# Key weights in four transfers, corrected keys piece by piece, more products on zeros in the last stage, a new order table

## Chip, cores and metric

One core of one Trainium2 chip runs the kernel. The metric is the device time of one execution in microseconds, as the median of several runs.

## What is computed

Two layers, each a linear-attention block A and a sparse gated MLP block B with a residual around each, on x of 2048 rows by 512 columns (bf16). Cut to what matters:

```python
def _A_ref(x, wqkv, wo):                     # H = 32 heads of 16
    q, k, v = split(x @ wqkv)
    phi = lambda t: jnp.where(t > 0, t + 1, jnp.exp(t)) + 1e-6
    pq, pk = phi(q), phi(k)
    kv = jnp.einsum("bhsd,bhse->bhde", pk, v)
    z = jnp.einsum("bhsd->bhd", pk)
    num = jnp.einsum("bhqd,bhde->bhqe", pq, kv)
    den = jnp.einsum("bhqd,bhd->bhq", pq, z)[..., None] + 1e-6
    return (num / den).merge_heads() @ wo

def _B_ref(x, w_r, w_gate, w_up, w_down):
    r = x @ w_r
    idx = jnp.argsort(-r, axis=-1)[:, :2]            # the two rows with the largest logit
    y = (silu(x[idx] @ w_gate) * (x[idx] @ w_up)) @ w_down * sigmoid(r[idx])
    return x with y added to the rows idx

x = A_x
for layer in (1, 2):
    x = x + _A_ref(layernorm(x), A_wqkv, A_wo)
    x = x + _B_ref(layernorm(x), B_w_r, B_w_gate, B_w_up, B_w_down)
```

## The kernel before

The 2048 rows are 16 tiles of 128 rows (`NT`), the 512 columns four pieces of 128 (`NC`). All of x stays on the chip.

**Start.** The host hands in x twice, by rows (`x`) and transposed (`xt`), and the key weights `wk` ([128, 4, 512], 512 KB). `wk` comes in two transfers of 256 KB: pieces 0 and 1 on ScalarE's queue, 2 and 3 on SyncE's. TensorE first runs nine products on a tile of zeros (`spin`, L858) that give nothing but activity. The layer norm's mean is taken out of the key weights, not out of x: `center_keys` multiplies the four pieces of `wk` by a matrix of -1/512 (`nmean`, L872) into one PSUM tile, ScalarE copies it out as `wl` (L875), and four additions give the corrected pieces `wkc` = `wk` + `wl` (L877). Tile 0 doesn't wait for `wkc`: `K_raw(0)` multiplies `xt` by `wk` and adds `xt` by `wl` in the same PSUM tile (L416, L422). From tile 1 on `K_raw` uses `wkc`. Its result is scaled by the row's reciprocal deviation in two passes of ScalarE (`e`, L389, and `rl`, L390), and becomes `pk` by two passes of VectorE or GpSimd. The PSUM tiles of these products ("mm") rotate through three buffers.

**Body.** `G` (L434) sums xn times pk over the 16 tiles in four PSUM tiles, `Q` (L449) makes the queries in 16 groups of four products, `kv` turns the sums into per-head matrices (L488, L500, L530), `den` makes the denominators (L547 to L571), `O` (L587) the block's output, which VectorE adds to x (L592). The two chosen rows of block B of the first layer are worked out beside this (L986 to L1311).

**Last stage.** Once the second layer's x is there, the two rows are searched in parts: the tiles 0 to 11 first (`topk`, L986 to L995), then 12 to 15 (L1438, L1450), then all (L1452). `WL` (L1457) holds weights that pick the two rows; products with it (L1468, L1476) gather them into `xg2`, from which VectorE makes `xoT` and `xs` (L1484). Then come the rows of the output (L1524), gate and up (L1493) and down (L1533), and `yo` (L1546), stored over the two rows by the last two transfers (L1550), which wait for the four stores of the whole output (L1353). Each store takes four tiles of `xo` (written as `pk` in the rows), which are scaled copies of x made by `last_out` on ScalarE (L321), VectorE or GpSimd (L323). In three pauses TensorE multiplies zeros (`hot`, L1406): four, two and three products of 128 by 512.

**Order.** `Plan` records every operation with its engine. The string `ORDER` then lists them two characters each, and the operations are issued in that order, so it fixes the order within every engine and every queue. `PICK` names, for each operation that several engines can do, the one that does it. A GpSimd operation marked `port` waits for the VectorE operation marked `port` that stands last before it in the table; the code adds that wait itself.

## Time and profile before

| | |
|---|---|
| median of 3 runs | 154.9 us (154.62 to 155.18) |
| time of the profiled execution | 154.57 us |
| its span, first to last instruction | 152.9 us |
| TensorE busy | 145.0 us, 95% of the span |
| VectorE busy | 125.7 us, 82% |
| ScalarE busy | 110.3 us, 72% |
| GpSimd busy | 44.8 us, 29% |
| mean granted clock of TensorE | 0.978 |

The profile is of one execution. Busy time of TensorE counts products that overlap, so a full share doesn't mean that none of it could be shorter. The end of a stretch is set by the wait that ends last in it, and the chain of waits follows these back from the last instruction.

### The profile page before, as it was taken

How to read it: one execution, taken by the hardware profiler on the slowest of the kernel's cores; microseconds unless marked ns; L12 is line 12 of the kernel's file. 1: busy time of each engine (PE TensorE's matmuls, PEld its weight loads, DVE VectorE, ACT ScalarE, POOL GpSimd, SP SyncE). 2: the span in 40 equal slices, each digit the busy share in tenths (PEclk: the TensorE clock that was granted, in tenths of full speed). 3: DMA queues.
4: the chain of work that ended last, by engine and by line, in shares of the span. 5: the costliest groups of instructions: out<-in, count | busy, mean ns of one | idle time of the engine just before them, and what ended most of it. 6: DMA issues, size and time to landing. Idle time of an engine off the chain costs nothing.

```text
span 152.9 us, 3774 instructions
## 1 busy us (share of the span) xinstructions
PE 145.0 (95%) x1296; PEld 73.6 (48%) x1313; DVE 125.7 (82%) x455; ACT 110.3 (72%) x268; POOL 44.8 (29%) x102
## 2 busy tenths in 40 slices
PE   7999999999999999999999999999999999997790
PEld 2344444454445444444444455665546554554490
DVE  0499999849798999999999588676499999989930
ACT  3279999697277786798987565133877998989930
POOL 7623514341104442504500031210341144562100
PEclk9999999999999999999999999999999999999965
DMA  4999999959991000379553510000000000040380
GB/s 117 361 265 382 313 299 258 79 108 333 206 321 60 0 4 0 69 130 422 135 109 71 103 34 0 6 0 4 0 0 4 0 4 0 0 137 9 137 274 5
DMA packets 23155, 18.20 MB, mean 119 GB/s; under 512 B 18016, under 2 KB 20576, under 8 KB 22752
## 3 DMA queue, kind: packets, MB, share of 16 engines
q1 hardware_dynamic: 22840, 17.57, 42.6%
q10 hardware_dynamic: 296, 0.39, 0.8%
q8 instruction: 10, 0.16, 0.4%
q14 instruction: 9, 0.07, 0.2%
HBM read 11.67 MB, written 2.10 MB: 90 GB/s over the span
## 4 chain that ended last, share of the span: by engine, by line
PE 74%; DVE 16%; ACT 4%; issue 3%; DVEq 0%; ACTq 0%
PE g L434 17%; PE mm L449 16%; PE g L587 9%; PE mm L402 9%; DVE x L592 7%; PE mm L416 6%; PE tp L858 3%; DVE pq L571 2%; ACT e L389 2%; PE tp L1069 1%; PE g L1493 1%; ACT rl L390 1%; PE g L488 1%; PE g L872 1%; DVE x L1295 1%
## 5 line engine op out<-in xcount | busy, mean ns | idle before, releaser
L371 ACT ACTIVATE e<-mm 128x512 bf16<-128x512 f32 x48 | 28.2, 600 | 12.7 <-PE mm L402 7.1
L434 PE MATMUL g<-pk,xn 128*128 128x512 bf16 x125 | 31.2, 379 | 0.2
L449 PE MATMUL mm<-xnT,wq 128*128 128x512 bf16 x119 | 30.9, 379 | 0.4
L587 PE MATMUL g<-KW,pq 128*128 128x512 bf16 (+2 forms) x129 | 30.1, 372 | 0.2
L607 ACT ACTIVATE sq<-x 128x512 bf16<-128x512 bf16 (+2 forms) x31 | 18.8, 609 | 1.8 <-DVE x L592 1.6
L434 PEld LDWEIGHTS <-xn 128*128 128x128 bf16 x128 | 12.3, 98 | 13.7
L587 PEld LDWEIGHTS <-pq 128*128 128x128 bf16 x132 | 12.3, 98 | 13.3
L449 PEld LDWEIGHTS <-wq 128*128 128x128 bf16 x128 | 11.6, 97 | 13.3 <-issue 0.6
L379 POOL TENSOR_TENSOR pq<-rl,em 128x512 bf16<-128x512 bf16 x7 | 8.1, 1153 | 28.0 <-DVE em L375 23.4
L375 DVE TENSOR_SCALAR em<-e 128x512 bf16<-128x512 bf16 x48 | 13.1, 288 | 3.9 <-ACT e L371 3.6
L402 PE MATMUL mm<-wk,xnT 128*128 128x512 bf16 x63 | 16.0, 379 | 0.1
L416 PE MATMUL mm<-wkc,xt 128*128 128x512 bf16 x59 | 14.3, 379 | 0.1
L334 DVE BATCH_NORM_STATS2 st<-x 128x6 f32<-128x512 bf16 x16 | 10.5, 680 | 4.4 <-DMA x<-in_A_x_dram 4.4
L390 ACT ACTIVATE rl<-mm,rho 128x512 bf16<-128x512 f32 x16 | 11.0, 704 | 1.1 <-issue 1.1
L389 ACT ACTIVATE e<-mm,rho 128x512 bf16<-128x512 f32 x16 | 10.8, 699 | 1.1 <-PE mm L422 1.0
L592 DVE SCALAR_TENSOR_TENSOR x<-x,opr,g 128x512 bf16<-128x512 bf16 (+2 forms) x17 | 11.3, 711 | 0.0
L382 DVE SCALAR_TENSOR_TENSOR pk<-mm,em 128x512 bf16<-128x512 f32 x16 | 11.0, 688 | 0.2
L382 DVE SCALAR_TENSOR_TENSOR pq<-mm,em 128x512 bf16<-128x512 f32 x16 | 10.7, 686 | 0.2
L592 DVE SCALAR_TENSOR_TENSOR x<-x,g 128x512 bf16<-128x512 bf16 x16 | 10.5, 681 | 0.0
L416 PEld LDWEIGHTS <-xt 128*128 128x128 bf16 x64 | 6.3, 98 | 7.9 <-issue 0.7
L374 ACT ACTIVATE rl<-mm 128x512 bf16<-128x512 f32 x16 | 9.1, 596 | 1.3 <-PE mm L449 1.1
L323 POOL TENSOR_SCALAR xn<-x,s,nb 128x512 bf16<-128x512 bf16 x8 | 6.5, 821 | 10.6 <-DVE nb L357 9.9
(294 smaller groups left out, 242.2 us busy)
## 6 DMA issues: line engine op xcount, KB each, us to landing
wgu<-in_B_wgu_dram SPq DMA_DIRECT2D x2, 1408.0 KB, 6.5
out_dram<-pk SPq DMA_DIRECT2D x4, 512.0 KB, 3.0
wd<-in_B_wd_dram SPq DMA_DIRECT2D x1, 1408.0 KB, 6.7
xt<-in_A_xt_dram SPq DMA_DIRECT2D x2, 512.0 KB, 8.1
x<-in_A_x_dram SPq DMA_DIRECT2D x2, 512.0 KB, 9.9
xt<-in_A_xt_dram SPq DMA_DIRECT2D x3, 256.0 KB, 3.7
x<-in_A_x_dram SPq DMA_DIRECT2D x3, 256.0 KB, 4.6
wq<-in_A_wq_dram SPq DMA_DIRECT2D x1, 512.0 KB
```

Of the source, the lines that this page charges most:

```text
L371: act(0.5, lambda: A.activation(out=e()[:], in_=p()[:], func=ACT.Exp), r=[p], w=[e], **k)
L375: dve(0.2, lambda: V.tensor_scalar(out=em()[:], in0=e()[:], scalar1=1.0, scalar2=TINY, op0=ALU.min, op1=ALU.add), r=[e], w=[em], port=True ...
L382: dve(0.6, lambda: V.scalar_tensor_tensor(out=out_ap, in0=p()[:], scalar=0.0, in1=em()[:], op0=ALU.max, op1=ALU.add), r=[p, em], w=[key], **k)
L389: act(0.57, lambda: A.activation(out=e()[:], in_=p()[:], func=ACT.Exp, scale=s_), r=[p, ("rho0", t)], w=[e])
L390: act(0.57, lambda: A.activation(out=rl()[:], in_=p()[:], func=ACT.Relu, scale=s_), r=[p, ("rho0", t)], w=[rl])
L402: T_.matmul(p()[:], lhsT=xnT[:, c, t * P : (t + 1) * P], rhs=wk[:, c, :], start=(c == 0), stop=(c == NC - 1))
L416: T_.matmul(p()[:], lhsT=xt[:, t, c, :], rhs=w_[:, c, :], start=(c == 0), stop=(c == NC - 1 and not raw))
L434: T_.matmul(Gs[c]()[:], lhsT=xn[:, t, gcol(c) : gcol(c) + P], rhs=pk[:, t, :], start=first, stop=last)
L449: T_.matmul(p()[:], lhsT=wq[:, i, c, :], rhs=xnT[:, i, j * D : (j + 1) * D], start=(i == 0), stop=(i == NC - 1))
L587: T_.matmul(p()[:, 0:n], lhsT=pqt(c, t * P, P), rhs=KWs[layer][:, c, a : a + n], start=(c == 0), stop=(c == NC - 1),)
L592: dve(0.07 + 0.6 * n / D, lambda a=a, n=n, p=p, h=h: V.scalar_tensor_tensor(out=x[:, t, a : a + n], in0=x[:, t, a : a + n], scalar=1.0 if ...
L607: A.activation(out=sq()[:, 0:n], in_=xh, func=ACT.Square, scale=float(D) ** -0.5, accum_out=acc)
```

## The change

- `wk` comes in four transfers of 128 KB, one for each piece, alternating between ScalarE's queue (0 and 2) and SyncE's (1 and 3). Each of the four products with `nmean` then needs one piece.
- The seven products on zeros at the start were nine.
- `K_raw(1)` is issued as four products of their own (L424 in the new file), each behind its piece of `wkc`.
- In the last stage the third pause has five products on zeros in place of three, and three more (`hot4`) stand between the gathering products and the output's rows, which name `hot4` as something to come after.
- `ORDER` and `PICK` are new throughout. Across the whole kernel VectorE has three fewer copies out of PSUM (L315, 7 to 4), two fewer of `last_out` (5 to 3), one fewer of each of the norm and the `wkc` additions, two more additions of pq (9 to 11) and one more square with its sum. ScalarE has three more of the copies, GpSimd two more of `last_out` and one `wkc` addition.

The diff, without most of the tables:

```diff
 ORDER = (
-    "0P8b000Q01030R020e05060708090A0X0B0k3x040Y450S0W0V0Z0f0T0a0g0U0b0r0l463y0y0m0c0h0i0n0w0C170s0o0t0z0D0E0H0F1D0G0x"
...
+    "00010R420S4403020406050708090A0B0C0D0E0T0F0G0J8f0Z0U0m0a0n0b0o0c4A0W4B0V0X0g0p0h0Y0t0j0d0u0q0v0i0w1C0x13110y0r12"
...
-    dma(wk[:, 0:2, :], A_wk[:, 0:2, :], [("wk", 0)], 256, eng="ACT")
+    for c in range(NC):
+        dma(wk[:, c : c + 1, :], A_wk[:, c : c + 1, :], [("wk", c)], 128, eng=("ACT", "SP")[c % 2], prio=-70.0 + c)
     x_load(0, 1, eng="ACT")
     xt_load(0, 1, 0.0, prio=-60.0)
-    dma(wk[:, 2:4, :], A_wk[:, 2:4, :], [("wk", 2)], 256, prio=-59.0)
...
+        def f1(c):
+            T_.matmul(p()[:], lhsT=xt[:, t, c, :], rhs=wkc[:, c, :], start=(c == 0), stop=(c == NC - 1))
+        if t == RAW:
+            for c in range(NC):
+                pe(MM, lambda c=c: f1(c), r=[("xt", t), ("wkc", c)], w=[p])
+        else:
+            pe(4 * MM, f, r=[("xt", t)] + r, w=[p])
...
-            pe(2 * MM, lambda k=k: f(k), r=[("wk", k)], w=[p])
+            pe(2 * MM, lambda k=k: f(k), r=[("wk", k), ("wk", k + 1)], w=[p])
...
-    spin(9)
+    spin(7)
...
-    hot(3, ["gE"], "hot3")
+    hot(5, ["gE"], "hot3")
...
-    pe(1.05, f, r=["WL", "onesb", "hot3"] + [("x", t) for t in (*range(LO, NT), "E")], w=[xg2]).st = 0.02
+    pe(1.05, f, r=["WL", "onesb", "hot3"] + [("x", t) for t in (*range(LO, NT), "E")], w=[xg2, "gW"]).st = 0.02
+    hot(3, ["gW"], "hot4", 2)
...
-    pe(0.15, f, r=["xoT", "masks0"], w=[yp])
+    pe(0.15, f, r=["xoT", "masks0", "hot4"], w=[yp])
```

VectorE at the start, before: statistics of the first two tiles (`st`), the four additions for `wkc`, and what follows.

```order
L334 BN_STATS st<-x 128x6 x2
L336 BN_AGGR mv<-st 128x2
L877 TENSOR_TENSOR wkc<-wk,wl 128x512 x4
L357 SCALAR_TENSOR_TENSOR nb<-mv,rho 128x1
L336 BN_AGGR mv<-st 128x2
L831 CAST blockmask<-mm 128x128
```

And now:

```order
L334 BN_STATS st<-x 128x6 x2
L336 BN_AGGR mv<-st 128x2 x2
L837 CAST blockmask<-mm 128x128
L883 TENSOR_TENSOR wkc<-wk,wl 128x512 x3
L357 SCALAR_TENSOR_TENSOR nb<-mv,rho 128x1 x2
```

The second tile's statistics and a mask are now ahead of the additions, of which three are left; the fourth (piece 1) is GpSimd's.

VectorE in the last stage, before: from the weights `WL` to the reciprocal of the gate's sigmoid. L323 are tiles of `xo`, L1484 `xoT` and `xs`, L1002 and L1006 the rows' indices.

```order
L1457 SCALAR_TENSOR_TENSOR WL<-keys,s_193,sc 128x45 x2
L323 TENSOR_SCALAR pk<-x,opr,nb 128x512 x4
L1484 TENSOR_REDUCE xoT<-tp 128x4x2
L1484 TENSOR_REDUCE xs<-tp 128x8
L323 TENSOR_SCALAR pk<-x,opr,nb 128x512
L1002 TENSOR_SCALAR s_194<-s_193 128x2
L1006 SCALAR_TENSOR_TENSOR s_195<-s_194 128x1
L1509 TENSOR_SCALAR s_198<-s_197 128x2
```

And now:

```order
L1463 SCALAR_TENSOR_TENSOR WL<-keys,s_193,sc 128x45 x2
L323 TENSOR_SCALAR pk<-x,opr,nb 128x512
L1008 TENSOR_SCALAR s_194<-s_193 128x2
L1012 SCALAR_TENSOR_TENSOR s_195<-s_194 128x1
L323 TENSOR_SCALAR pk<-x,opr,nb 128x512
L1491 TENSOR_REDUCE xoT<-tp 128x4x2
L1491 TENSOR_REDUCE xs<-tp 128x8
L323 TENSOR_SCALAR pk<-x,opr,nb 128x512
L1516 TENSOR_SCALAR s_198<-s_197 128x2
```

Between `WL` and `xoT` stand two tiles of `xo` and the two index operations, where four tiles of `xo` stood. The two tiles ahead are tiles 12 and 8; the one behind `xs` is tile 9, of the store that is issued last (tiles 8 to 11; before, tiles 12 to 15 were last).

GpSimd at its end, before: halves of the scales (L1343, L1344) and the key of the early candidates (L1431, L1432).

```order
L1343 CAST sc<-rho 128x3
L1344 TENSOR_TENSOR sc<-rho,sc 128x3
L1431 TENSOR_TENSOR s_185<-cand,eyg 128x2
L1432 TENSOR_TENSOR keys<-s_185 128x1
L1620 UNCONDITIONAL_BRANCH
```

And now:

```order
L1349 CAST sc<-rho 128x3
L1350 TENSOR_TENSOR sc<-rho,sc 128x3
L1437 TENSOR_TENSOR s_185<-cand,eyg 128x2
L1438 TENSOR_TENSOR keys<-s_185 128x1
L323 TENSOR_SCALAR pk<-x,opr,nb 128x512
L1627 UNCONDITIONAL_BRANCH
```

A tile of `xo` (tile 11, of the last store) now stands at GpSimd's end. In the table the VectorE operation marked `port` that stands last before it is tile 8 of `xo`.

## Rows read from the trace of the kernel before

**Rows 1.** Windows; columns: stretch, us, busy (instructions) by engine, clock, DMA.
```profile
14.60:116.40 101.80, 101.02 (x808) 50.65 (x820) 86.98 (x304) 74.67 (x177) 26.91 (x45) 1.00 0.48 118
116.40:138.20 21.80, 21.64 (x253) 11.58 (x245) 21.16 (x65) 19.45 (x55) 9.43 (x19) 1.00 0.07 25
138.20:143.90 5.70, 4.17 (x48) 1.75 (x44) 5.53 (x42) 5.40 (x18) 1.40 (x7) 1.00 0.12 39
143.90:149.40 5.50, 4.71 (x161) 4.27 (x161) 2.80 (x14) 2.69 (x5) 0.00 (x0) 0.71 0.74 253
```

**Rows 2.** Chain of waits, in order of time; columns: start us, us, what.
```profile
1.06 4.02 PE tp L858 x9
...
143.89 1.29 DVE pk L323 x4
```

**Rows 3.** Timeline, 0 to 14 us: start, us, engine, line, operation.
```profile
4.97 1.64 PE L872 MATMUL g<-wk,nmean 128*128 128x512 bf16 x4
...
6.44 1.03 PE L416 MATMUL mm<-wk,xt 128*128 128x512 bf16 x4
6.64 0.60 ACT L875 ACTIVATE wl<-g 128x512 bf16<-128x512 f32 x1 [3.61 <-PE g L872]
...
7.27 1.43 DVE L877 TENSOR_TENSOR wkc<-wk,wl 128x512 bf16<-128x512 bf16 x4 [0.33 <-ACT wl L875]
...
8.44 2.85 PE L416 MATMUL mm<-wkc,xt 128*128 128x512 bf16 x12
```

**Rows 4.** DMA issues: tiles, queue, count, KB each, median us to landing.
```profile
out_dram<-pk SPq DMA_DIRECT2D x4, 512.0 KB, 3.0
...
wk<-in_A_wk_dram SPq DMA_DIRECT2D x1, 256.0 KB, 3.9
wk<-in_A_wk_dram ACTq DMA_DIRECT2D x1, 256.0 KB, 4.1
```

**Rows 5.** Timeline, 112 to 134 us.
```profile
115.56 0.69 DVE L375 TENSOR_SCALAR em<-e 128x512 bf16<-128x512 bf16 x3
...
116.19 0.41 PE L547 MATMUL tp<-pq,Z 128*32 128x128 bf16 x16
...
118.89 0.68 DVE L315 CAST KW<-g 128x512 bf16<-128x512 f32 x1
...
133.27 0.77 POOL L323 TENSOR_SCALAR pk<-x,opr,nb 128x512 bf16<-128x512 bf16 x1
```

**Rows 6.** Timeline, 134 to 153 us.
```profile
140.19 0.40 PE L990 MATMUL tp<-identf,s 128*128 128x128 f32 x2 [0.89 <-DVE s L986]
...
142.64 0.82 PE L1406 MATMUL g<-warm 128*128 128x512 bf16 x3
...
143.80 1.38 DVE L323 TENSOR_SCALAR pk<-x,opr,nb 128x512 bf16<-128x512 bf16 x4
...
144.50 0.24 PE L1476 MATMUL tp<-WL,xt 128*128 128x6 bf16 x4
...
145.35 0.24 PE L1524 MATMUL g<-ident,xoT 128*32 128x128 bf16 x4 [0.62 <-DVE xoT L1484]
...
147.91 1.37 PE L1533 MATMUL g<-wd,h 128*32 128x128 bf16 x44
...
149.33 0.29 DVE L1546 CAST yo<-g 128x128 bf16<-128x128 f32 x1 [1.14 <-PE g L1533]
```

**Rows 7.** Windows of half a microsecond, columns as in Rows 1.
```profile
146.00:146.50 0.50, 0.50 (x26) 0.50 (x23) 0.04 (x1) 0.41 (x2) 0.00 (x0) 0.69 1.03 338
146.50:147.00 0.50, 0.50 (x25) 0.50 (x23) 0.13 (x1) 0.15 (x1) 0.00 (x0) 0.50 1.01 336
```

**Rows 8.** Timeline of SyncE's queue, 145.6 to 150 us.
```profile
145.77 0.37 SPq L1353 DMA_DIRECT2D out_dram<-pk  x1
149.87 0.71 SPq L1550 DMA_DIRECT2D out_dram<-yo  x1
```

**Rows 9.** SyncE's waits: who, for whom, us, times, longest.
```profile
SPq L1550 <- DMA out_dram<-pk: 2.0, 1, 2.0
```

51 lines of the change are left out of this document (25 added, 26 removed).

## The prediction

> **What bounds the kernel now.** I read the windows first, then the chain of waits, then the timelines at both ends, where the chain leaves TensorE. From 14.6 to 116.4 us TensorE is busy for 101.02 of 101.80 us, so at most 0.8 us can be won there without removing products, and the change removes none there. From 116.4 to 138.2 us VectorE is nearly as full (21.16 of 21.80 us) beside a full TensorE, and from 138.2 to 143.9 us VectorE leads (5.53 of 5.70 us). In the last stretch the granted clock is 0.71 on average [rows 1]. The chain begins with the nine products on zeros, 4.02 us from 1.06 us, and near the end it passes through four VectorE tiles of `xo` (L323), 1.29 us [rows 2]. So the parts to price are the start up to the corrected keys, the balance between TensorE and VectorE around 116 us, and the last 6 us.
>
> **The start.** The nine products take 4.02 us, 0.45 us each, and the first product of the means starts at 4.97 us; its four take 1.64 us, and from 6.44 us four products take 1.03 us and twelve 2.85 us, 0.24 us each [rows 2, 3]. By this pace TensorE is at the lower of its two levels (1.2 GHz) until about 6.2 us and at the upper (2.4 GHz) after, though it has worked since 1.06 us. Seven products on zeros end at 1.06 + 7 x 0.45 = 4.2 us. The means can't start before their key pieces land: the two 256 KB transfers land 3.9 and 4.1 us after issue, a 512 KB store in a quiet time takes 3.0 us [rows 4]. So the first two pieces may come as late as before (4.97 us) or a good microsecond sooner. I take a start at 4.3 us, nearer to the early end because only half of the bytes stand before them. That is 0.67 us of TensorE time at half pace, worth 0.33 us of later time if the pace changes where it did; bounds 0 and 0.8.
>
> The Trainium skill (DMA: Bandwidth & Descriptors, Anatomy of one DMA) fits a transfer on the GpSimd path by 2.0 us plus bytes over 436 GB/s: most of it doesn't shrink with the size. By that the first pieces land 0.3 us sooner, and the term is 0.15 us. The 3.9 and 4.1 us here are far above the 2.6 us that the fit gives for 256 KB; no row shows 128 KB of weights.
>
> What follows the means is `wl` (0.60 us on ScalarE, from 6.64 us), then four additions on VectorE from 7.27 us, 1.43 us or 0.36 us each [rows 3]. `wl` comes earlier, but VectorE now does the second tile's aggregation and the mask ahead of the additions, so they begin near 7.2 us all the same. Three take 1.07 us; the fourth, on GpSimd, costs 0.77 us (a one-input pass of that size, [rows 5]) to about twice that, and begins some 0.6 us ahead of VectorE's. The piecewise product of tile 1 hides the rest: before, it began at 8.44 us with the additions ending at 8.70 us, now its first piece is there by 7.6 us and its last by 8.4. If GpSimd's piece holds the others up, the term of 0.33 us is lost. I take -0.35 us for the start in all, the bounds being -0.8 and +0.1. SyncE's queue gets one more issue, but the loads behind it wait for the same bytes as before, and what is moved behind transposes (rows 12 to 15 of x) isn't used for another ten microseconds.
>
> The Trainium skill (SBUF — State Buffer, SBUF: two separate sides) says that GpSimd and a VectorE pass with two SBUF inputs share one port pair, which the first to start holds until it ends. By that GpSimd's addition makes VectorE's three wait, and the start wins nothing. No row here shows the two in such a pass together.
>
> **The body.** Products and their count are the same. Across the kernel VectorE gives away three PSUM copies (0.68 us each, [rows 5]) and gets some back; where TensorE leads, this is worth nothing. In the second layer eight products of `Q`, two groups, are moved behind the last `G`. The sums of `G` are ready 8 x 0.24 = 1.9 us sooner, and so is all of `kv` behind them, less what else is moved ahead of it. Against that stand VectorE's passes for these two groups, which now fall into its full stretch: twice an em of 0.69/3 = 0.23 us [rows 5] and an addition of about 0.4 us, 1.3 us. I take 0 for the body: -0.8 if all of TensorE's idle time there goes, +1.3 if VectorE's passes come on top.
>
> **The last stage.** The two added products of the third pause take 0.43 us at 0.215 us each. The pause is 0.44 us: its three products end at 142.64 + 0.82 = 143.46 us, and the next start behind `WL` at 143.9 us [rows 2, 6]. They are just hidden; if `WL` comes sooner, they cost up to 0.4 us. The three of `hot4` take 0.65 us from about 144.6 us, when the last gathering product has started (144.50 us and three more), so until 145.25 us. The output's rows started at 145.35 us, 0.62 us idle, waiting for `xoT` [rows 6]. `xoT` itself stood behind four tiles of `xo`, 1.38 us; now two tiles (0.69 us) and two index passes (about 0.2 us each), so it is ready 0.3 us sooner. Of this `hot4` leaves 0.1 us.
>
> Behind that the clock matters. It was granted at 0.69 from 146.0 to 146.5 us and at 0.50 after [rows 7], behind pauses of 0.44 and 0.62 us and products of few columns. Earlier in the stage pauses of up to 0.89 us [rows 6], with products on zeros between them, left it at 1.00 [rows 1]. Five more of these in the two pauses should hold it. The 44 products of the down projection took 1.37 us at 0.50; 16 of the same form took 0.41 us at the upper level [rows 5, 6], which makes 44 x 0.41/16 = 1.13 us, and twice the clock can at most halve the 1.37. So the clock is worth 0.24 to 0.69 us there; I take 0.45. The gate and up products have two columns each, for which I take nothing. `yo`, ready at 149.33 + 0.29 = 149.62 us [rows 6], would be ready 0.55 us sooner, at 149.07.
>
> The last transfers wait for the stores as well. The last store was issued at 145.77 us and the last transfer at 149.87 us [rows 8], after 2.0 us in which SyncE waited for stores [rows 9]; so `yo` and the last store came almost together, and `yo` alone gains nothing. The last store now needs tile 9 (VectorE, behind `xs`, about 145.5 us) and tile 11 on GpSimd, 0.77 us [rows 5] behind VectorE's tile 8 (143.9 + 0.35 + 0.4 + 0.35 = 145.0 us), so 145.8 us: issued as before. But the store ahead of it (tiles 12 to 15) is issued sooner, so it may land after 3.0 us [rows 4], at 148.8 us, and not at 149.7. The gain of the stage lies between 0 and 0.65 us; I take 0.35.
>
> **Sum.** -0.35, 0 and -0.35 make -0.7 us. The profiled execution took 154.57 us, 152.9 of it its span; it becomes 153.9. It lies 0.33 us under the median of the runs, 154.9 us, so the median becomes 154.2 us.
>
> **Rivals.**
> - The gains are hidden at both ends: GpSimd's addition delays tile 1, and tile 9 of `xo` waits for GpSimd's tile 11 (to 145.8 + 0.35 us), so the last store lands no sooner than before. For it: `yo` and the store stand together in [rows 8, 9]. Against it: the store's landing depends on the store ahead, which is now earlier. Time: 154.9 less 0.1, 154.8 us. This is what the port rule named above would make of it.
> - Slower, by VectorE after 116 us: the two moved groups of `Q` put 1.3 us of its passes behind `kv`, where it has 0.64 us idle in 21.8 [rows 1]. It decides once `kv` comes less than 1.3 us sooner, for instance since its four PSUM copies now wait in ScalarE's queue. With the full price, the start's 0.35 us kept and nothing from the last store: 154.9 + 1.3 - 0.35 = 155.85, some 155.8 us. Against it: the copies that VectorE no longer does.
> - Faster: the new order also takes out the 0.8 us in which TensorE idles from 14.6 to 116.4 us, or most of it, and VectorE follows with its lighter load: 154.2 less 0.8, 153.4 us. Against it: those 0.8 us are spread over 100 us.
> - The clock falls all the same. Then `yo` is 0.1 us sooner in place of 0.55; the time is 154.45 us, within the forecast's own range.
>
> **Chances.** The forecast, with the case of the clock, 0.43 (its own range 153.6 to 154.8 us); hidden gains 0.18; slower 0.22; faster 0.17. A difference under 0.3%, 0.46 us, can't be told from no change. Faster than 154.44 us: 0.30 of the forecast's 0.43, 0.03 of the hidden, all 0.17, so 0.50. Slower than 155.36 us: 0.19 of the slower case and 0.01 of the rest, 0.20. The same: 0.30. For 8 times in 10 the range runs from 153.0 us (the fast case with the start's better bound in part) to 155.6 us.
>
> **What would show it.** The start is right if the first product of the means begins at 4.2 to 4.4 us and `G`'s first at least 0.3 us sooner than its place before; wrong if TensorE pauses after the seventh product on zeros for more than 0.3 us, or if VectorE's additions wait for GpSimd's. The body is right if VectorE's first addition into x of the second layer stands no later than before against the end of `kv`. The last stage is right if the granted clock is still 1.00 during the down projection, `hot4` ends by the time `xoT` is ready, and the last transfer waits for a store. A median above 155.4 us would make the forecast wrong as such, and so would one under 153.6 us, which would mean that the order and not the named edits moved the time.

## The result and the profile after

The changed kernel is slower: 155.92 us in the median of 16 runs (155.3 to 156.93) against 155.04 us of the kernel before in as many runs beside it (153.85 to 155.61). The ratio is 1.0062, with a 95% interval from 1.0037 to 1.0086. The forecast of 154.2 us and its range (to 155.6 us) are both missed. The profiled execution took 155.49 us and its span 153.7 us, against 154.57 and 152.9 us.

The windows of the changed kernel, columns as in [rows 1]:

```profile
14.60:116.40 101.80, 100.72 (x822) 50.78 (x836) 85.98 (x305) 75.90 (x180) 22.30 (x41) 1.00 0.51 116
116.40:138.20 21.80, 21.64 (x225) 11.31 (x227) 21.42 (x70) 20.12 (x57) 10.86 (x20) 1.00 0.07 25
143.90:149.40 5.50, 4.47 (x164) 3.66 (x160) 2.66 (x12) 2.58 (x5) 0.77 (x1) 0.93 0.57 193
146.00:146.50 0.50, 0.50 (x26) 0.50 (x23) 0.15 (x1) 0.31 (x2) 0.00 (x0) 1.00 1.02 338
146.50:147.00 0.50, 0.50 (x26) 0.50 (x23) 0.21 (x2) 0.19 (x1) 0.00 (x0) 1.00 0.79 246
```

The two long stretches look as they did. In the last 5.5 us the granted clock has risen from 0.71 to 0.93, and where it stood at 0.69 and 0.50 [rows 7] it is 1.00.

The start, on the timeline (start us, us, engine, line, operation):

```profile
1.06 3.17 PE L864 MATMUL tp<-warm 128*128 128x512 bf16 x7 [1.06 <-DVE warm L218]
4.02 1.65 PE L878 MATMUL g<-wk,nmean 128*128 128x512 bf16 x4
5.71 0.60 ACT L881 ACTIVATE wl<-g 128x512 bf16<-128x512 f32 x1 [2.20 <-PE g L878]
5.77 1.04 PE L416 MATMUL mm<-wk,xt 128*128 128x512 bf16 x4
6.39 1.15 POOL L883 TENSOR_TENSOR wkc<-wk,wl 128x512 bf16<-128x512 bf16 x1 [1.14 <-ACT wl L881]
7.57 1.09 DVE L883 TENSOR_TENSOR wkc<-wk,wl 128x512 bf16<-128x512 bf16 x3
8.04 1.05 PE L424 MATMUL mm<-wkc,xt 128*128 128x512 bf16 x4 [0.37 <-DVE wkc L883]
8.92 2.75 PE L416 MATMUL mm<-wkc,xt 128*128 128x512 bf16 x12
```

The means start at 4.02 us (before 4.97) and `wl` at 5.71 (6.64), both some 0.9 us sooner [rows 3]. But VectorE's additions begin 0.3 us later and TensorE waits 0.37 us for them. Tile 1's products (L424) start at 8.04 us; before, they were the first four of the twelve that start at 8.44. So 0.40 us of the 0.9 are left there.

The last stage, on the timeline:

```profile
142.44 1.25 PE L1412 MATMUL g<-warm 128*128 128x512 bf16 x5
143.16 0.51 DVE L1463 SCALAR_TENSOR_TENSOR WL<-keys,s,sc 128x45 bf16<-128x45 f32 x2
144.38 0.81 PE L1412 MATMUL g<-warm 128*128 128x512 bf16 x3
144.70 0.77 POOL L323 TENSOR_SCALAR pk<-x,opr,nb 128x512 bf16<-128x512 bf16 x1 [1.58 <-DVE pk L323]
144.76 0.85 DVE L323 TENSOR_SCALAR pk<-x,opr,nb 128x512 bf16<-128x512 bf16 x1
145.29 1.95 PE L1500 MATMUL g<-xs,wgu 128*128 128x2 bf16 x72
147.57 0.80 PE L1540 MATMUL g<-wd,h 128*32 128x128 bf16 x44
148.42 0.29 DVE L1553 CAST yo<-g 128x128 bf16<-128x128 f32 x1 [0.58 <-PE g L1540]
```

SyncE's queue at the end, its longest wait there, and the times from issue to landing of the four stores:

```profile
145.77 0.37 SPq L1359 DMA_DIRECT2D out_dram<-pk  x1
150.71 0.71 SPq L1557 DMA_DIRECT2D out_dram<-yo  x1
```
```profile
SPq L1557 <- DMA out_dram<-pk: 3.2, 1, 3.2
```
```profile
DMA to landing us min/median/max: 2.9/3.0/4.8
```

The down projection takes 0.80 us in place of 1.37 [rows 6], and `yo` is there at 148.71 us, 0.91 us sooner. Yet the final transfer is issued at 150.71 us, 0.84 us later than before [rows 8]. The last store is issued at 145.77 us in both kernels; its landing took 3.9 us before and takes 4.8 us now, and SyncE's wait for it has grown from 2.0 us [rows 9] to 3.2.

Three marks divide the time: the end of the first layer's last `G` product, about 42 us ("`G` ends" below); the first `WL` pass; the issue of the final transfer. A mark is fair only if both kernels have done the same work up to it. The end of the last key product, about 32 us, is not: the twenty small products with `wr` (L837 and L842 before, L843 and L848 now), 0.5 us, stood behind it and now stand ahead of it. Up to the last `G` product both orders issue the same products, as a count of every TensorE record of e3 and e5 (below) shows. Before, then after:

```profile
33.85 0.54 PE L837 MATMUL mm<-wr,wot 128*128 128x1 bf16 x16
38.66 3.62 PE L434 MATMUL g<-pk,xn 128*128 128x512 bf16 x16
```
```profile
30.94 0.54 PE L843 MATMUL mm<-wr,wot 128*128 128x1 bf16 x16
40.08 1.89 PE L440 MATMUL g<-pk,xn 128*128 128x512 bf16 x8
```

| | `G` ends | to `WL` | `WL` to final issue |
|---|---|---|---|
| before | 42.28 | 101.10 | 6.49 |
| after | 41.97 | 101.19 | 7.55 |
| difference | -0.31 | +0.09 | +1.06 |

So the final transfer's 0.84 us are the last stage alone: in these two executions the start gains 0.31 us and the body loses 0.09.

### The profile page after: what moved, and what is told of

It is laid out like the page before. It is cut to its first block, busy times and chain, and to the rows that moved or that the text cites. A ratio compares the mean times of both kernels' runs of the same rounds, so it can differ in the third digit from the quotient of the medians.

```text
span 153.7 us, 3756 instructions
## 1 busy us (share of the span) xinstructions
PE 144.6 (94%) x1298; PEld 73.1 (48%) x1316; DVE 124.0 (81%) x454; ACT 112.5 (73%) x270; POOL 44.0 (29%) x101
## 4 chain that ended last, share of the span: by engine, by line
PE 76%; DVE 13%; DMA 3%; issue 2%; ACT 2%; ACTq 1%; DVEq 0%
PE g L440 18%; PE mm L455 17%; PE g L593 9%; PE mm L402 9%; PE mm L416 8%; DVE x L598 6%; DMA x<-in_A_x_dram 3%; ACT sq L613 2%; PE tp L1075 1%; DVE pq L577 1%; PE g L494 1%; PE tp L553 1%; PE g L1500 1%; PE g L1412 1%; DVE x L1301 1%
## 5 line engine op out<-in xcount | busy, mean ns | idle before, releaser
L593 PE MATMUL g<-KW,pq 128*128 128x512 bf16 (+2 forms) x129 | 29.6, 372 | 0.3 <-issue 0.2
L375 DVE TENSOR_SCALAR em<-e 128x512 bf16<-128x512 bf16 x48 | 13.6, 294 | 7.7 <-ACT e L371 6.6
L613 ACT ACTIVATE sq<-x 128x512 bf16<-128x512 bf16 (+2 forms) x30 | 18.3, 610 | 1.3 <-DVE x L598 1.1
L416 PE MATMUL mm<-wkc,xt 128*128 128x512 bf16 x56 | 13.5, 379 | 0.0
L598 DVE SCALAR_TENSOR_TENSOR x<-x,g 128x512 bf16<-128x512 bf16 x16 | 10.8, 682 | 0.9 <-PE g L593 0.8
L598 DVE SCALAR_TENSOR_TENSOR x<-x,opr,g 128x512 bf16<-128x512 bf16 (+2 forms) x17 | 11.2, 712 | 0.1
L323 POOL TENSOR_SCALAR xn<-x,s,nb 128x512 bf16<-128x512 bf16 x7 | 5.3, 768 | 19.9 <-DVE em L375 7.6
L577 DVE TENSOR_TENSOR pq<-pq,rd 128x1024 bf16<-128x1024 bf16 x14 | 9.4, 685 | 0.1
L402 PEld LDWEIGHTS <-xnT 128*128 128x128 bf16 x64 | 6.0, 98 | 7.1 <-issue 0.6
```

Source lines behind the costliest of these rows:

```text
L375: dve(0.2, lambda: V.tensor_scalar(out=em()[:], in0=e()[:], scalar1=1.0, scalar2=TINY, op0=ALU.min, op1=ALU.add), r=[e], w=[em], port=True ...
L402: T_.matmul(p()[:], lhsT=xnT[:, c, t * P : (t + 1) * P], rhs=wk[:, c, :], start=(c == 0), stop=(c == NC - 1))
L416: T_.matmul(p()[:], lhsT=xt[:, t, c, :], rhs=w_[:, c, :], start=(c == 0), stop=(c == NC - 1 and not raw))
L577: pl.any({"DVE": (0.6, True), "POOL": (2.25, True)}, lambda e, q=q: EL[e].tensor_tensor(out=q, in0=q, in1=rd()[:].to_broadcast([P, 2, D]), ...
L593: T_.matmul(p()[:, 0:n], lhsT=pqt(c, t * P, P), rhs=KWs[layer][:, c, a : a + n], start=(c == 0), stop=(c == NC - 1),)
L598: dve(0.07 + 0.6 * n / D, lambda a=a, n=n, p=p, h=h: V.scalar_tensor_tensor(out=x[:, t, a : a + n], in0=x[:, t, a : a + n], scalar=1.0 if ...
```

## What held the store

In the stores' tail the trace has a packet of another queue. DMA by queue (packets, MB, share of 16 engines), of the changed kernel from 148.5 to 149 us, then from 149.5 to 150 us:

```profile
GB/s 0 0 1311 0 0 0 0 0 0 0 0 0 0 0 0 0 0 0 0 0 0 0 0 0 0 0 0 0 0 0 0 0 0 0 0 0 0 0 0 0
q8 instruction: 1, 0.02, 11.9%
```
```profile
q1 hardware_dynamic: 4, 0.00, 6.1%
```

The kernel before, from 149 to 149.5 us:

```profile
GB/s 0 0 82 0 0 82 0 0 0 82 0 0 0 1311 0 0 0 0 0 0 0 0 0 0 0 0 0 0 0 0 0 0 0 0 0 0 0 0 0 0
q8 instruction: 1, 0.02, 11.8%
```

Each figure of GB/s is for a fortieth of the window. The large packet, 16 KB of code, holds one DMA engine for 11.9% of 16 x 0.5 us, 0.95 us. Before, it starts at 149.16 us, right behind the last 1 KB packets of the store (82 GB/s). Now it starts at 148.53 us, nothing runs beside it, and the store's last six 1 KB packets follow from 149.46 to 150.0 us, each as the one before it ends. That they wait on the same engine is read from these times; the trace doesn't name a packet's engine.

I had three theories. **A:** TensorE's next piece of code is called when TensorE leaves its last product; a faster last stage calls it sooner. **A2:** the piece is called at a fixed place in TensorE's program, well ahead of its use, and cuts in when TensorE passes that place early against the last store. **B**, the rival to both: the earlier third store or GpSimd's tile 11 slows the last one.

**Products behind the last product** (e1 after, e2 before; A: TensorE stays busy, the piece comes late, the store lands after 3.9 us).

```diff
+    hot(5, [], "hot5")
```

(`hot5` stands last in the table.)

> The changed kernel with five products on zeros (128x512) behind TensorE's last useful product; nothing waits for them. Theory A: TensorE fetches a piece of code when it leaves its last product; in the changed kernel that piece (16 KB on one DMA engine, 0.95 us) starts at 148.55 us, ahead of the last packets of the last store, which then lands at 150.6 instead of about 149.3, and the two final transfers wait for it. Five products take about 1.05 us at full clock, so the fetch starts at about 149.5, behind the store's tail: the final transfers are issued at about 149.3 to 149.4, the profiled span ends 1.2 to 1.4 us earlier than the changed kernel's, and the time is 154.4 to 154.8 against 155.0 of the kernel before. Rival B: the store lands late for a reason of its own (memory, receipt), or what ends last is something else: the time stays at 155.7 to 156.0, the final issue 2 us behind yo. Rival C: the added work at TensorE's end costs by itself: over 156.

> The kernel before with the same five products on zeros behind its last useful product. Theory A: there the code piece starts at 149.16 us, just behind the last packet of the last store (landed 149.67, yo ready 149.62), so there is hardly anything to win: 0 to -0.3 us (the gain only in executions in which the piece comes a little sooner), 154.7 to 155.1. Rival C (work at TensorE's end helps or costs by itself, through the clock or the end of the program): the same shift as in the changed kernel with these products, over 0.7 us either way.

e1 took 156.18 us (ratio to before 1.0085, 1.0053 to 1.0117), its final transfer 7.44 us behind `WL`, the piece again at 148.66 us. e2 took 154.92 us (0.9994, 0.9962 to 1.0025), 6.48 us. (Each ratio is to the kernel before as it ran beside that experiment.) Nothing moved: A is wrong. e1 also shows that the clock is not sure to hold: with the changed kernel's products ahead of it, its down projection was granted 0.50 of the clock and took 1.37 us.

```profile
148.14 1.37 PE L1540 MATMUL g<-wd,h 128*32 128x128 bf16 x44
```

**The named products alone, in the kernel before** (e3, and e4 with `hot5` as well).

```diff
-    hot(3, ["gE"], "hot3")
+    hot(5, ["gE"], "hot3")
...
+    hot(3, [], "hot4")
```

> The kernel before with only the products on zeros of the change: five instead of three in the third pause, three in the new fourth pause; the weights, the start and the order of the rest are as before. Theory A: yo comes 0.5 to 0.8 us sooner since the clock holds, but the code piece of TensorE also comes that much sooner (148.4 to 148.7) and meets the tail of the last store, which is issued at 145.77 as before: it lands at 150.4 to 150.9, so the time gets worse by 0.7 to 1.2 us, to 155.7 to 156.2. Rival B (the late landing belongs to the new order of the stores and of the output tiles): the store lands at 149.7 as before, which was level with yo, and the time is 154.8 to 155.1. What I predicted of these products (-0.35): 154.7.

> The kernel before with the change's products on zeros and, behind TensorE's last useful product, five more. Theory A: the code piece starts at about 149.6, behind the store's tail; the store then lands at 149.3 to 149.7 and ends the wait: 154.7 to 155.1, level with the kernel before or up to 0.3 us below it, and 0.7 to 1.2 us below the same kernel without the five products. Rival B: no difference from that kernel.

e3's `yo` and its final transfer:

```profile
148.63 0.29 DVE L1546 CAST yo<-g 128x128 bf16<-128x128 f32 x1 [0.57 <-PE g L1533]
149.84 0.71 SPq L1550 DMA_DIRECT2D out_dram<-yo  x1
```

`yo` is 0.70 us sooner than before and the transfer leaves as before: 154.71 us, ratio 0.9989 (0.9956 to 1.0021); e4 154.65 us, 1.0002 (0.9964 to 1.0039). The products hold the clock here (1.00 in the down projection, which takes 0.80 us) and it is worth nothing, for the store ends last. By themselves they don't make the store late: so far B stood better than A, which had forecast 155.7 to 156.2 us for e3.

**A2 from both sides.** Between the starts of two successive pieces lie 199 to 399 records of TensorE before and 131 to 408 after, 268 on average in both; one spacing in each is exactly 256 (records 1222 to 1478 before, 686 to 942 after). The Trainium skill (Runtime: NRT & Kernel Launch, Instruction fetch mechanics) says that an engine's code is refilled in blocks of 256 instructions by a DMA queue of its sequencer's own, and that crossing a block's boundary is "mostly hidden". The averages are near the first, and e6 below disagrees with the second as far as a store is concerned: it waits for the piece. If the place is fixed, two things follow that look wrong otherwise: more work on the chain to `yo` should make the changed kernel faster (e5), and splitting products on zeros at the start, 141 us ahead, should make the kernel before slow (e6). The edits of e5, in the changed kernel, and of e6, in the kernel before (36 products of 128 columns for 9 of 512):

```diff
-    hot(3, ["gW"], "hot4", 2)
+    hot(5, ["gW"], "hot4", 2)
```
```diff
-            for _ in range(n):
-                T_.matmul(
-                    p()[:].rearrange("p (a d) -> p a d", a=NC), lhsT=warm[:, 0, :], rhs=warm[:].to_broadcast([P, NC, P]),
...
+            for a in range(4 * n):
+                a = a % 4 * P
+                T_.matmul(p()[:, a : a + P], lhsT=warm[:, 0, :], rhs=warm[:, 0, :], start=True, stop=True)
```

> The changed kernel with five instead of three products on zeros in the fourth pause, 0.45 us more on TensorE's chain. The five products at the program's end did not move the code piece (it started at 159.65 against 159.78 on the trace's own clock), so it isn't called at TensorE's end but from a place inside the last stretch, and it cuts into the last store in the changed kernel (landing 4.8 us) and in that variant (4.7), where the 72 gate products start 0.48 and 0.43 us ahead of the store's issue; where they start 0.12 to 0.2 us ahead (the kernel before and its three variants) the piece comes behind the store's last packet and the landing is 3.9. Theory A2: it is this lead of TensorE over the last store that decides. Two more products take the lead away (0.45 us), the piece falls behind the store, which lands about 3.5 us after its issue, at 149.3; yo is ready at 149.15: 154.5 to 154.9, that is 1.0 to 1.4 below the changed kernel, by adding work to its longest chain. Rival B2: the new order of the stores makes the landing 4.8: 155.8 to 156.1, yo hidden behind it. Rival C: TensorE's chain ends last: 156.3.

> The kernel before with each of its nine products on zeros at the start (128x512) as four of 128x128: the same columns, 54 more TensorE instructions ahead of everything else. Theory A2: pieces of TensorE's code are 256 instructions, so the last piece is called 54 instructions sooner within the gate products, which run at about 27 ns for two instructions, 0.7 us sooner; it then cuts into the last store as in the changed kernel, whose order of stores this kernel does not have: landing 4.6 to 4.9 us instead of 3.9, time 155.7 to 156.1 against 155.0. Rival B2 (order of stores): landing 3.9, 154.9 to 155.2. If the split products take longer at the start, that shows in the first 6 us and is to be taken off.

e5: `yo` is a full microsecond later than in the changed kernel (0.44 us by the two products, 0.57 by a down projection that took 1.37 us at a granted clock of 0.50) and the final transfer 0.93 us sooner.

```profile
149.46 0.29 DVE L1553 CAST yo<-g 128x128 bf16<-128x128 f32 x1 [1.14 <-PE g L1540]
149.78 0.70 SPq L1557 DMA_DIRECT2D out_dram<-yo  x1
```

Its DMA from 148.5 to 149 us shows the piece behind the store's packets again, as before:

```profile
GB/s 0 0 0 0 82 0 0 0 0 0 82 0 0 0 82 0 0 0 82 0 0 82 0 0 0 1311 0 0 0 0 0 0 0 0 0 0 0 0 0 0
q8 instruction: 1, 0.02, 11.8%
```

e5 took 154.82 us, ratio to before 1.0033 (1.0003 to 1.0064), 6.62 us behind `WL`. e6 took 155.8 us, 1.0078 (1.0044 to 1.0111), 7.52 us behind `WL`. Its zeros at the start take the 4.02 us of before, its piece falls into the midst of the last store, from 147 to 147.5 us, and that store lands after 4.9 us (the final transfer leaves at 150.84 us):

```profile
1.06 4.02 PE L859 MATMUL tp<-warm 128*128 128x128 bf16 x36 [1.06 <-DVE warm L218]
```
```profile
q8 instruction: 1, 0.02, 13.9%
```
```profile
DMA to landing us min/median/max: 2.9/3.1/4.9
```

e6 has neither the changed stores nor GpSimd's tile 11 nor a held clock, and it has the whole loss. That is A2, and against B. Since splitting TensorE's products moved the piece, the queue is TensorE's.

Nine kernels have whole stores and no split zeros, and they fall into line by the lead of the gate products' start over the last store's issue: a lead of 0.48 and 0.49 us (after, e1) goes with landings of 4.80 and 4.69 us, 0.24 us (before, e2, e3, e4) with 3.89, and 0.05 us (e5 and, below, e10 and e12) with 3.55 and 3.56. What the traces don't show is the call itself. The piece starts 4.21, 4.98 and 5.37 us behind `WL` in e7 (below), e1 and after, whose TensorE programs are the same up to there, and within 0.02 us of the end of the store's last packet in before, e2, e3, e4, e5, e8, e10 and e12. So its start depends on the stores, and that the place of the call is fixed in the program is argued, not shown.

**Away from the piece.** e18 splits all zeros of the changed kernel, which puts more instructions into the program and other ones where its pieces begin; e7 and e8 send the last two stores as four of 256 KB (e7 in the changed kernel, with tiles 12 and 15 of `xo` exchanged between ScalarE and VectorE; e8 in e3's kernel); e9 adds the split to e7, e14 to e8. The products of `spin` have 92 columns there (45 of 102 in e14), those of `hot` four times 128.

```diff
-    spin(7)
+    spin(39)
```
```diff
-            store(t - 3, t + 1)
+            store(t - 3, t + 1 if t < 11 else t - 1)
...
-    store(LO, NT)
+    store(LO + 2, NT)
...
+    store(10, 12, "o2")
+    store(12, 14, "o2")
```

> The changed kernel with its last two stores (tiles 12 to 15, 8 to 11) as four of two tiles each, issued as their tiles are ready (12 and 13, 14 and 15, 10 and 11, 8 and 9), and tiles 12 and 15 exchanged between ScalarE and VectorE so that 12 and 13 are ready at about 143. The data of the last two stores (1 MB, 3.1 us at 340 GB/s) can then start at about 143.9 instead of 145.0. Theory A or A2 (the last store's landing ends the wait in the changed kernel, yo has been ready for 2 us): the last piece lands by about 148.6, yo (148.7) ends the wait: final issue at about 148.9 to 149.2, time 153.8 to 154.4. If the code piece still cuts into the last 256 KB: 154.6 to 155.0. Rival (the final transfers wait for something else than data): 155.8.

> The kernel before with the change's products on zeros and its last two stores as four of two tiles each, in the order 8, 10, 12, 14. Without the pieces yo was ready at 148.6 and the store landed at 149.8, level with the kernel before. With the wait for the store gone, yo ends it: 0.6 to 1.0 us less, 154.0 to 154.4. The difference to the changed kernel with pieces is then what the change's start, body and order are worth: by the prediction 0.35 us for it, by the trace's idle time of TensorE 0.2 us for it. Rival (the products only move the wait): 154.7 to 155.0.

> The changed kernel with its last two stores as four of two tiles each, as in the run before, and with all products on zeros cut finer (the seven at the start into 39 of 92 columns, the eleven and three of the pauses into four of 128 columns each): the same columns, 130 more TensorE instructions ahead of the gate products. From the start of VectorE's WL passes to the issue of the final transfers it took 7.55 us in the changed kernel, 6.50 in the kernel before, 7.03 with the four store pieces alone, where the code piece cut into the last of them with 17 packets to go. Theory A2 (the place of TensorE's code fetch against the stores): with 130 more instructions the piece is called among the 20 small products ahead of the gate, about 1.1 us after WL, and comes between the store pieces instead of in the last one; yo, ready 5.55 us after WL, then ends the wait: 5.7 to 6.1 us from WL to the final issue, 1.0 to 1.3 less than with the pieces alone; time 154.1 to 154.6. Rival: the stores are limited by their data alone and the piece does not matter: 7.0 from WL, 155.5. If the finer products hold the clock less well, gate products of over 2.0 us and a clock below 1 before 148 show it.

> The kernel before with the change's products on zeros in the last stage, the last two stores as four of two tiles, and all products on zeros cut finer (138 more TensorE instructions ahead of the gate products). Start, body and order table are otherwise those of the kernel before. The last stage then has what the changed kernel has with the same two cures (5.85 us from WL to the final issue, 154.43); what is left between them is the worth of the change's start, body and order. By the prediction (start -0.35, body 0) this kernel is 0.35 us slower than that one; by the WL times of the profiles so far (143.5 in the mean of both families) they are level: from WL to the final issue 5.8 to 6.1 us, 154.2 to 154.7.

> The changed kernel with the products on zeros cut finer and nothing else (130 more TensorE instructions ahead of the gate products, the two last stores whole). In the runs with both cures the code piece that cut into the last store came 1.5 to 2.1 us behind WL, ahead of the stores' data, and the program, now over 2,700 TensorE instructions long, called one more at 5.3 to 5.8 us behind WL. Theory A2: the store, whose data lay between 1.9 and 5.5 us behind WL, is left alone by the first and met at most at its end by the second: from WL to the final issue 6.1 to 6.4 us instead of 7.55, 154.5 to 155.0. If the second comes ahead of the last packets: 7.0 to 7.5, 155.5 to 156. Rival (only the pieces of the stores helped): 155.9.

| | median us | ratio to before (95%) | `G` ends | `WL` to final issue |
|---|---|---|---|---|
| e7 after, stores in pieces | 155.74 | 1.0061 (1.0031 to 1.0092) | 43.19 | 7.03 |
| e8 before, products, pieces | 155.05 | 1.0026 (0.9989 to 1.0063) | 43.28 | 6.07 |
| e9 after, pieces, split | 154.43 | 1.0003 (0.9975 to 1.0031) | 42.08 | 5.85 |
| e14 before, products, pieces, split | 154.84 | 1.0022 (0.9992 to 1.0053) | 41.62 | 6.79 |
| e18 after, split | 155.02 | 1.0042 (1.0013 to 1.0071) | 43.54 | 6.29 |

e18 has 11 pieces. Two fall into its last stage: one at 146.22 us, ahead of the third store's first packet (146.6), and one at 149.98, beside the last store's last packets. That one holds nothing up: 12 packets follow in the next half microsecond, 0.04 us apart as without a piece. So a piece beside a store's end need not cost anything. No store takes over 3.9 us, and the stage is 1.26 us shorter than after's. In e9 the stage is the shortest of the five, 0.64 us under before's:

```profile
148.54 0.29 DVE L1549 CAST yo<-g 128x128 bf16<-128x128 f32 x1 [0.58 <-PE g L1536]
149.11 0.71 SPq L1553 DMA_DIRECT2D out_dram<-yo  x1
```

e14's stage takes 6.79 us. Its 11th piece starts at 148.31 us, in the last store, but that store lands after 2.97 us, as in e9 (2.93). It is issued late, 3.67 us behind `WL` (e8 2.42, e9 2.79): SyncE's issue of the store ahead of it, at 144.58 us, took 1.70 us in place of 0.45 in e8, beside the tenth piece (144.36 us, 1.53 us long). Whether the piece was the reason stays open. e9 is faster than the changed kernel and level with the one before; no version beat both.

## Where the start and the body went

With the last stage mended (e9's is 0.64 us shorter than before's), the 0.35 us predicted ahead of it should show as well, and e9's ratio of 1.0003 says that the two together don't. The marks of all profiled executions separate the start from the body.

- From the end of `G` to `WL` takes 101.08 to 101.10 us in all seven kernels with the order of before, and 101.17 to 101.20 us in the ten that have the new order of the body; e10 and e11, which alter it, are below. So the new body takes 0.1 us more.
- `G` ends at 41.62 to 43.28 us, on average 42.31, in the seven kernels with the start of before, and at 41.79 to 43.54 us, on average 42.43, in the seven with the start of after. With one execution each and a spread (standard deviation) of 0.55 and 0.68 us, neither a gain of 0.35 us nor a loss as large can be ruled out by these. The medians, each less what its profile's last stage differs from before's, give an estimate for start and body together against before: -0.1 us in the changed kernel, but +0.4 to +0.9 in e1, e5, e7, e9 and e18; with the old order -0.2 to +0.2, and +0.8 in e8. By these a loss is likelier than a gain.

What TensorE waits for between 2 and 33 us (waits over 0.15 us): with the start of before nothing in before, e2, e3, e4, e6 and e14, and once 0.6 us for ScalarE's `rl` in e8. With the start of after only the 0.37 us for `wkc` in after, and nothing in e9; but in e5 and in e18 (us in total, times, longest; two of e18's four):

```profile
PE mm L424 <- DVE wkc L883: 0.3, 1, 0.3
PE mm L455 <- DMA xnT<-xn: 0.2, 1, 0.2
PE mm L416 <- DMA xt<-in_A_xt_dram: 0.2, 1, 0.2
```
```profile
PE mm L455 <- DMA xnT<-xn: 1.1, 1, 1.1
PE g L440 <- DVE pk L394: 0.6, 1, 0.6
```

So TensorE, sent off 0.9 us sooner, catches up with VectorE's additions, the loads of x and the transposes behind them, and gives some of the time back there, in some executions all of it. In after, 0.40 us are left at tile 1 and 0.31 at the end of `G`.

Several of these waits were attacked by an edit of their own: additions ahead of tile 1's statistics (e12), x ahead of the second key pieces on each queue (e13), the keys in two transfers again (e15), the fourth addition back on VectorE with a `G` product ahead of the first `Q` (e16). e12 and e10 stand on e5; e13, e15 and e16 on e9; e11 has the pieces, the split, e10's and e12's moves. As the engines' orders, VectorE's in e12:

```diff
-L334 BN_STATS st<-x 128x6 x2
-L336 BN_AGGR mv<-st 128x2 x2
+L334 BN_STATS st<-x 128x6
+L336 BN_AGGR mv<-st 128x2
+L883 TENSOR_TENSOR wkc<-wk,wl 128x512 x3
 L837 CAST blockmask<-mm 128x128
-L883 TENSOR_TENSOR wkc<-wk,wl 128x512 x3
```
ScalarE's queue in e13 (SyncE's likewise):

```diff
-L186 DMA wk<-in_A_wk_dram 128x512 x2
+L186 DMA wk<-in_A_wk_dram 128x512
 L186 DMA x<-in_A_x_dram 128x512
+L186 DMA wk<-in_A_wk_dram 128x512
```

e15's loads:

```diff
-    for c in range(NC):
-        dma(wk[:, c : c + 1, :], A_wk[:, c : c + 1, :], [("wk", c)], 128, eng=("ACT", "SP")[c % 2], prio=-70.0 + c)
+    dma(wk[:, 0:2, :], A_wk[:, 0:2, :], [("wk", 0), ("wk", 1)], 256, eng="ACT")
+    dma(wk[:, 2:4, :], A_wk[:, 2:4, :], [("wk", 2), ("wk", 3)], 256)
...
```

VectorE in e16, and in e10, which moves the first layer's gather corrections (products, a copy, two passes of L1301) ahead of `KVm`, to use that TensorE reaches `KV` early:

```diff
+L881 TENSOR_TENSOR wkc<-wk,wl 128x512
 L837 CAST blockmask<-mm 128x128
 L881 TENSOR_TENSOR wkc<-wk,wl 128x512 x3
```
```diff
-L506 TENSOR_TENSOR KVm<-g,blockmask 128x512
...
 L1301 TENSOR_TENSOR x<-x,mm 128x512
+L506 TENSOR_TENSOR KVm<-g,blockmask 128x512
```

> The changed kernel with five products on zeros in the fourth pause (154.82 when run before) and the two corrections of x by the gathered rows (two small transposes, two products of 512 columns, one small copy and two VectorE passes of 0.7 us) moved from about 118 to 123.5 us up to 112 to 116 us, ahead of VectorE's KVm pass. Theory V: TensorE reaches the second layer's last KV product 0.9 us sooner than in the kernel before (114.2 to 115.1), VectorE then stands idle for 0.7 to 0.9 us around 113 to 115.4, and afterwards is busy without a gap up to 140, with those two passes in the stretch; the first addition to x comes no sooner (123.55 to 123.35). With them in the gap, KVm comes 0.6 to 0.7 us later but 1.75 us of passes leave the stretch: the WL passes start 0.6 to 1.0 us sooner, time 153.8 to 154.4. Rival T (TensorE or ScalarE sets the stretch, VectorE only follows): no gain or a loss of 0.6 us from the products put ahead of the KV product: 154.7 to 155.5.

> The changed kernel with the store pieces and the finer products on zeros of the first run of this group, the moved corrections of the second and the moved key passes of the fourth. If the three theories hold and add up: WL 0.9 to 1.4 us sooner than in the changed kernel, the final issue 5.7 to 6.1 us behind it: 153.0 to 153.8. If only the stores' part holds: 154.1 to 154.6.

> The changed kernel with five products on zeros in the fourth pause (154.82 when run before) and VectorE's three additions to the key weights moved ahead of the statistics of x tile 1 (with the aggregate of tile 0 ahead of them and that of tile 1 behind). Theory S: in the changed kernel the means end 1.5 us sooner (wl at 5.1 to 5.7 instead of 6.6), but VectorE takes two statistics passes of x first and begins the additions at 7.1 to 7.6, as in the kernel before (7.3), so TensorE waits 0.3 to 0.5 us at 7 us. With the additions ahead, the corrected keys' products start at 7.0 to 7.3 instead of 7.6 to 8.0 and that idle time goes; 0.3 to 0.5 us less at WL: 154.3 to 154.6. Rival: the statistics of x tile 1, later by 1.1 us, hold the first exponentials and the PSUM buffers back: idle time at 9 to 12 us, no gain or up to 0.5 us lost: 154.8 to 155.3.

> The changed kernel with the four store pieces and the finer products on zeros (154.43 when run before), and with the loads of x tiles 0 and 1 ahead of the second piece of the key weights on ScalarE's and SyncE's queues. In the changed kernel VectorE starts its first statistics when x tile 0 lands (5.4 to 6.0 us), ends them and their aggregates at about 7.0 and only then adds the means to the keys (7.1 to 7.6), though wl is there at 5.7; TensorE waits for it 0.3 to 0.5 us. Theory S2 (the landing of x sets VectorE's start): x tile 0 lands 0.8 to 1.2 us sooner, the statistics lie ahead of wl, the additions begin at 5.9 to 6.3, the means 0.2 to 0.4 us later than now; TensorE's wait at 7 us goes, the first exponentials come 0.7 to 1 us sooner; 0.3 to 0.6 us less: 153.8 to 154.2. Rival: the means, later by two tiles' transfer (256 KB at 340 GB/s, 0.75 us), move everything: 154.8 to 155.2.

> The changed kernel with the four store pieces and the finer products on zeros (154.43), and with the key weights in two transfers of 256 KB, one on each queue, as in the kernel before, not in four of 128 KB; x tile 0 and xt tile 0 are issued one place sooner on their queues. Theory S3 (the four transfers bring the means sooner, but VectorE's statistics of x, held by x tile 0's later issue, begin the additions at the same time): the means end later, x tile 0 lands 0.2 to 0.4 us sooner, and the corrected keys' products start level or sooner: 154.2 to 154.5. Rival, as predicted: the means wait for whole transfers, 0.35 to 0.8 us lost: 154.8 to 155.2.

> The changed kernel with the four store pieces and the finer products on zeros (154.43), with the one key addition that the change gave to GpSimd back on VectorE, and with one group of G products ahead of the first query products, which wait 0.2 to 0.8 us for a DMA transpose at 23 to 25 us. Theory P (VectorE and GpSimd slow each other): VectorE's three additions took 1.09 us where GpSimd's was over before them, and 1.50, 1.61, 1.89 and 2.05 us where it lay beside them more and more; four on VectorE alone should take 1.43, as in the kernel before. Together with the query products' wait 0.3 to 0.6 us less: 153.8 to 154.2. Rival: the first exponentials or the landing of x hold TensorE anyway: 154.4 to 154.8.

| | median us | ratio to before (95%) | `G` ends | to `WL` |
|---|---|---|---|---|
| e10 gather's corrections early | 155.24 | 1.0055 (1.0027 to 1.0083) | 41.79 | 101.79 |
| e11 all | 156.55 | 1.0152 (1.0110 to 1.0194) | 43.11 | 101.79 |
| e12 additions first | 156.42 | 1.0098 (1.0059 to 1.0137) | 44.30 | 101.19 |
| e13 x first | 156.17 | 1.0102 (1.0061 to 1.0143) | 42.47 | 101.20 |
| e15 keys in two | 154.82 | 0.9999 (0.9964 to 1.0034) | 42.89 | 101.20 |
| e16 addition on VectorE | 155.46 | 1.0070 (1.0043 to 1.0097) | 43.33 | 101.18 |

None won anything. What their traces show is of one execution each, of e12 its slowest (157.02 us) and of e13 its fastest (154.31, 1.9 under its median), so for these two the reasons are hints. In e12 the first exponentials come late and hold their PSUM tiles:

```profile
11.44 1.02 PE L416 MATMUL mm<-wkc,xt 128*128 128x512 bf16 x4 [1.50 <-ACT e L389]
```

In e13 the second half of the means waits for its keys:

```profile
6.04 0.59 PE L876 MATMUL g<-wk,nmean 128*128 128x512 bf16 x2 [0.95 <-DMA wk<-in_A_wk_dram]
```

e15's ratio is level with e9's, so four transfers are worth nothing against two here. e16 waits 0.7 us for ScalarE's `xn`. In e10 `KVm` comes 1.0 us later (116.43 us, 115.43 in after), the first addition into x of the second layer (L598; 123.26 us, 81.47 from the end of `G`, 81.59 in after) is only 0.1 us sooner and waits 0.3 us for TensorE now, and the body takes 0.6 us more, in e11 as well: the corrections were not what kept TensorE's lead at `KV` from being used.

## Why the prediction was wrong

**The last stage is the step that failed**: "the store ahead of it (tiles 12 to 15) is issued sooner, so it may land after 3.0 us [rows 4], at 148.8 us, and not at 149.7". The last store landed at 150.6 us, 4.8 us after its issue. The store ahead was issued sooner (144.13 us, before 144.60) and it didn't help; the code piece cut in, which was in the page's list of queues (`q8 instruction`) and in no term of mine. The predicted -0.35 us is +1.06, of which the landing's growth is 0.9 us. The other two terms came out near their forecasts in this execution, so this one made the miss.

**The clock's term held in this execution and counted for nothing.** `yo` was to come 0.55 us sooner and came 0.91 sooner, 0.57 of it in the down projection (1.37 to 0.80 us, against 0.24 to 0.69 predicted; the 44 products took less than 44/16 of the 0.41 us of sixteen, so scaling by count made the lower bound too small). e3 gives 0.70 us for the products alone. But "Five more of these in the two pauses should hold it" is not sure: in e1, with the same products, the clock was 0.50 again. `yo` was ready at 149.62 us before and the transfer left at 149.87 [rows 6, 8], so even an undisturbed landing left nothing of this.

What did the harm was not the clock: e3 and e4 have its products and no loss, and in e1 the clock fell and the loss was there. It was TensorE's lead over the last store. `WL` comes 0.22 us sooner, and the gate products with it (145.29 us, before 145.53), but the store is issued at 145.77 us as before, since it waits for tile 9, which takes 0.85 us beside GpSimd's tile 11 and ends at 145.61. So the lead is 0.48 us in place of 0.24, and the code piece came early against the store. e5 gave the lead back (its gate products start at 145.72 us) and with it 0.93 us.

**The start.** The term of -0.35 us came out at -0.31 at the end of `G` in this execution. Its parts were off: the means started at 4.02 us, not 4.3, and `wl` came 0.93 us sooner, not 0.33, since the pace changed sooner too: the four means, about 0.43 us each, end at 5.67 us (before 6.61), and the key products behind them take half of that. (The granted clock reads 1.00 from 1 us on in both kernels; only the pace shows the change.) Against that, I had written "The piecewise product of tile 1 hides the rest", with its last piece there by 8.4 us: VectorE's three additions end at 8.66, and TensorE waits 0.37 us for them. Two errors of opposite sign made the sum, so its closeness is in part luck, and over the seven executions no gain shows.

**The body** was put at 0 and costs 0.1 us; the feared 1.3 us of VectorE's passes don't show. The slower rival gave 155.8 us, near the time that came, by the wrong mechanism. The rival with GpSimd's addition was wrong on the start in this execution (GpSimd's piece ends at 7.54 us, VectorE's first begins at 7.57). It was right that tile 9 and tile 11 keep the last store from being issued sooner, but its 154.8 us left out the piece that this let in.

**Still open**: where TensorE's program calls the piece, and why a piece holds the packets behind it in after and e6 and not in e18; whether the start of after gains or loses on average; which of VectorE and TensorE sets the time from 115 to 123.5 us; and whether e9 or e14 is the better start and order, whose ratios stand 0.2% apart.

## What to carry to other kernels

Before pricing a faster last stage, list everything that its final transfers wait for, and look at each DMA queue that is active between the last store's issue and its landing, the instruction queues too. Where a 16 KB piece of code falls into that stretch, a change in the number of instructions ahead of it in the program, or in how far an engine runs ahead of the store, can cost or give back a microsecond, as e6 and e5 did here; test with a kernel that changes only the count of instructions. Work sent off sooner at the start is a gain only as far as the next thing it needs comes sooner too. And where the order of work is new, compare times only at marks up to which both kernels have done the same work: at the last key product this start seems to lose 0.19 us and the body to gain 0.41, at the end of `G` the start gains 0.31 and the body loses 0.09.

## What was not expected of the hardware

- A piece of TensorE's code, 16 KB, takes 0.95 us as one packet where nothing runs beside it, and by their times the 1 KB packets of a store that are left behind it wait for it. The store of 512 KB lands after 4.8 or 4.9 us in place of 3.9, whether the piece starts near the store's end (148.53 us in after) or in its midst (147.39 in e6). In e18 a piece at 149.98 us held none of the packets beside it.
- VectorE's and GpSimd's additions of two SBUF inputs don't run side by side. Where GpSimd's (1.15 us) has started first, the one of VectorE's that meets it ends 0.28 us behind GpSimd's end, however long that makes it (0.94 us in e7, 1.22 in e15), and the other two take their usual 0.41. Where VectorE's has started first (e12, e13), GpSimd's takes 1.39 us. In ns, shortest, median and longest, in e7; then the timeline of e12:

```profile
L883 DVE TENSOR_TENSOR wkc<-wk,wl x3: 412/414/941, 7.1 to 8.3; 128x512 bf16<-128x512 bf16 x3
```
```profile
6.60 2.05 DVE L883 TENSOR_TENSOR wkc<-wk,wl 128x512 bf16<-128x512 bf16 x3 [0.28 <-ACT wl L881]
6.66 1.39 POOL L883 TENSOR_TENSOR wkc<-wk,wl 128x512 bf16<-128x512 bf16 x1 [1.39 <-ACT wl L881]
```

- Two key transfers of 128 KB land 2.7 and 3.1 us after issue, where 256 KB took 3.9 and 4.1 [rows 4], 1.0 to 1.2 us more. The fit of the Trainium skill (DMA: Bandwidth & Descriptors, Anatomy of one DMA), which is for the GpSimd path, would make the difference 0.3 us, an estimate from its figures; for these two queues the measurement decides.

```profile
wk<-in_A_wk_dram SPq DMA_DIRECT2D x2, 128.0 KB, 2.7
wk<-in_A_wk_dram ACTq DMA_DIRECT2D x2, 128.0 KB, 3.1
```
